# Attention and SoLU feed-forward on one core: a written order against an order set by a list schedule

## The chip, the core and the metric

The kernel runs on one core of a Trainium2 chip. A core has five engines, each with its own instruction queue worked strictly in order: TensorE (PE in the profile), VectorE (DVE), ScalarE (ACT), GpSimd (POOL) and SyncE (SP, which here only starts transfers). Engines wait for one another through semaphores; an instruction whose wait is not over holds up everything behind it on its engine. The metric is the device time of one execution in microseconds (us): 205.87 us in the median of three runs before the change (203.0 to 207.03).

## The reference

Attention over 4 batches of 8 heads (768 positions, 64 numbers per head), then a feed-forward block on the 3072 tokens of 512 numbers:

```python
scores = q @ k.T / sqrt(64) - slope[h] * dist     # kept: the last 96 positions and the first 8
a = softmax(scores);  x = a @ v                   # x as [3072, 512]
h = x @ w_in                                      # [3072, 1024]
solu = h * softmax(h)
ln = (solu - mean(solu)) / sqrt(var(solu) + 1e-6) * g_ln
out = ln @ w_out                                  # [3072, 512], float32
```

## The kernel before

The work is cut into 24 tiles of 128 tokens, six per batch. For a batch the q and k of two heads at a time (a pair, eight per batch) are loaded as float32 (`raw`), cast to fp16 by POOL (`qkn`, line 90), turned by six PE transposes into the PSUM bank `pt` (line 160) and copied out in order (`qkT`, line 164, q by DVE and k by ACT). Such a turn-and-copy is called a fill; there are 32. v is loaded per tile (`vst`) and cast by POOL (`vo`).

A tile n then goes through these steps. Scores of two halves on PE into `ps` (line 178), exp on ACT (`eb`, line 186; the first tile of a batch has half the width, line 189), times a mask on DVE (line 203), product with v on PE (`pav`, line 218), division by the sum on DVE (lines 233 and 237), four PE transposes (line 244) and a copy (`xT`). Feed-forward: eight 512-column matmuls on PE into `ph` (line 256), exp with row sum on ACT (`e`, line 268), `u = e*h` with row sum on DVE (line 274), a transposing transfer of u by SP (`uT`, line 279), squares with row sum on ACT (`sq`, line 285), five small POOL operations per two tiles for the factor `rs`, eight 512-column matmuls into `po` (line 308), scaling on ACT (`osb`, line 314), and the store, which ACT starts itself (line 316).

The mean of the normalisation is taken out of the weights beforehand: `gw_r = g * w_out` on ACT (line 323), its column mean by eight matmuls with a constant (`pm`, line 329), and `gw_sb = g * w_out - mean` on DVE (line 333). No `po` can start before that.

The order is written by hand: the loop over t at the end issues, for each t, the steps of several tiles in one fixed sequence (scores of t, feed-forward of t-2, output of t-4, store of t-5), with `gw_round` at t = 2 and 3, `gw_mean` and `gw_centre` at t = 4, and the fills of the next batch at the t that `FILLS` names. Loads of q, k and v are issued by SP, `w_in`, `w_out` and `g` by POOL (lines 356 to 359). PSUM has eight banks and all are taken: two each for `ps`, `pav` and `ph`, one for `pt` and one for `po`.

Of the kernel before, what the change touches and what calls it, by code (L numbers as in the profile page):

```python
# [9 lines left out]
FP32 = mybir.dt.float32  # L10
# [6 lines left out]
P = 128  # L17


@with_exitstack  # L20
def kernel(
# [24 lines left out]
    LAG = 4  # L46
# [14 lines left out]
    vo = const.tile([P, B, NA, H, D + 1], FP16, name="vo")  # L61
# [5 lines left out]
    vst = {}  # L67

    def load_v(n):
        b, a = divmod(n, NA)  # L70
        vst[n] = sb.tile([P, H, D], FP32, name="vst", bufs=4)
        nc.sync.dma_start(out=vst[n],
                          in_=v[b, :, ts(a, P), :].rearrange("h p d -> p h d"))

    def cast_v(n):
        b, a = divmod(n, NA)
        nc.gpsimd.tensor_copy(out=vo[:, b, a, :, 0:D], in_=vst.pop(n))  # L77

    raws, qkn = {}, {}

    def load_pair(b, w, pr):
        t = sb.tile([P, 2, NA * D], FP32, name="raw", bufs=10)
        nc.sync.dma_start(
            out=t, in_=(q, k)[w][b, 2 * pr : 2 * pr + 2].rearrange(
                "m (p a) d -> p m (a d)", a=NA))
        raws[b, w, pr] = t

    def cast_pair(b, w, pr):
        t = sb.tile([P, NA, 2, D], FP16, name="qkn", bufs=4)
        nc.gpsimd.tensor_copy(  # L90
            out=t.rearrange("p a m d -> p m a d"),
            in_=raws.pop((b, w, pr)).rearrange("p m (a d) -> p m a d", d=D))
        qkn[b, w, pr] = t

    with tc.manual_schedule():
        PAIRS = [(w, pr) for pr in range(NP) for w in range(2)]
        for i, (w, pr) in enumerate(PAIRS):
            load_pair(0, w, pr)
            if i == 3:
                load_v(0)  # L100
        load_v(1)
# [49 lines left out]
        qkT = {}  # L151

        def fill_pair(b, w, pr, tag="t"):

            if b not in qkT:
                qkT[b] = sb.tile([P, 2 * NP, S], FP16, name="qkT")
            pt = psum.tile([P, NA, P], FP16, name="pt", tag=tag)
            src = qkn.pop((b, w, pr))
            for a in range(NA):
                nc.tensor.transpose(  # L160
                    out=pt[:, a, :], in_=src[:, a].rearrange("p m d -> p (m d)"),
                    identity=ident)
            dst = qkT[b][:, w * NP + pr, :].rearrange("p (t a) -> p t a", a=NA)
            (nc.scalar.copy if w else nc.vector.tensor_copy)(  # L164
                out=dst, in_=pt.rearrange("p a t -> p t a"))

        ebs = {}

        def scores(n, half):
            b, a = divmod(n, NA)  # L170
            nb = 2 if a else 1
            ps = psum.tile([P, 2, 2, 2, P], FP32, name="ps", tag="s")
# [10 lines left out]
            eb = sb.tile([P, 2, 2, nb, P], FP16, name=f"eb{nb}", tag=f"eb{nb}", bufs=4)  # L183
            eb_f = eb.rearrange("p m s b f -> p (m s b f)")
            if nb == 2:
                nc.scalar.activation(out=eb_f, in_=ps.rearrange("p m s b f -> p (m s b f)"),  # L186
# [7 lines left out]
            if half == 1 and 1 <= a < NA - 1:  # L194

                nc.gpsimd.tensor_copy(out=qkT[b][:, NP : 2 * NP, ds(a * P, NG)],
                                      in_=qkT[b][:, NP : 2 * NP, 0:NG])
# [8 lines left out]

        pavs = {}

        def av(n, half):
# [5 lines left out]
            for i in range(4):  # L215
                m, slot = i % 2, i // 2
                for blk in range(nb):
# [3 lines left out]
                        rhs=vo[:, b, a - blk, 4 * half + i, :],  # L221
                        start=(i == 0 and blk == 0), stop=(i == 3 and blk == nb - 1),
                        skip_group_check=True)
            if half == 1 and 1 <= a < NA - 1:
                nc.gpsimd.tensor_copy(out=vo[0:NG, b, a], in_=vo[0:NG, b, 0])  # L225

        x16s, xTs = {}, {}
# [12 lines left out]
        def x_transpose(n):  # L240
            x16 = x16s.pop(n).rearrange("p g i d -> p (g i d)")
            pt = psum.tile([P, NCC, P], FP16, name="pt", tag="t")
            for c in range(NCC):
                nc.tensor.transpose(out=pt[:, c, :], in_=x16[:, ts(c, P)], identity=ident)
            xT = sb.tile([P, NCC, P], FP16, name="xT", bufs=3)
            nc.vector.tensor_copy(out=xT, in_=pt)
            xTs[n] = xT

        phs, es, us, uTs, sts, rss = {}, {}, {}, {}, {}, {}

        def ffn_in(n):
            xT = xTs.pop(n)
            ph = psum.tile([P, D_FF], FP32, name="ph", tag="h")
# [6 lines left out]
            phs[n] = ph  # L260

        def ffn_exp(n):
            if n % GT == 0:

                sts[n // GT] = stat.tile([P, 3, GT], FP32, name="st")
            i = n % GT
            es[n] = sb.tile([P, D_FF], FP16, name="e")
            nc.scalar.activation(out=es[n], in_=phs[n], func=AF.Exp,  # L268
                                 accum_out=sts[n // GT][:, 0, i : i + 1])

        def ffn_u(n):
            i = n % GT
            u = sb.tile([P, D_FF], FP16, name="u", bufs=3)
            nc.vector.scalar_tensor_tensor(  # L274
                out=u, in0=es.pop(n), scalar=1.0, in1=phs.pop(n),
                op0=ALU.mult, op1=ALU.mult,
                accum_out=sts[n // GT][:, 1, i : i + 1])
            uT = sb.tile([P, NFC, P], FP16, name="uT", bufs=LAG + 1)
            nc.sync.dma_start_transpose(out=uT, in_=u)
            us[n], uTs[n] = u, uT  # L280

        def ffn_sq(n):
            i = n % GT
# [167 lines left out]
```

## Time and profile before

| | before |
|---|---|
| profiled execution: time, span | 202.88 us, 201.1 us |
| busy: PE, PE weight loads | 148.8 us (74%), 81.0 us |
| busy: ACT, DVE, POOL | 131.9 us (66%), 115.5 us (57%), 83.9 us (42%) |
| moved by DMA | 34.85 MB, 173 GB/s in the mean |

How to read it: the span runs from the first to the last instruction, and the time of an execution has 1.8 us around it. Busy time is an average over stretches with different limits; the 40 digits of an engine cut the span in slices of 5.03 us, each digit the busy share in tenths. `PEclk` is the granted clock of TensorE in tenths of 2.4 GHz. The chain of waits follows the end of the span back: at each step to what released it, or to the instruction before it on its engine.

### The profile page before, as it was taken

The page shows a single profiled execution, that of the slowest core. Times are in us where ns is not written, and L with a number is a line of the kernel's source. Part 1 is how long each engine was busy: PE and PEld are TensorE (multiplying, and loading weights), DVE is VectorE, ACT ScalarE, POOL GpSimd, SP SyncE. Part 2 cuts the span into 40 slices and gives each one's busy share as a digit, 9 for nine tenths or more (in the row PEclk, how much of TensorE's full clock was granted, in tenths as well). Part 3 has the DMA queues.
Part 4 walks back from the last instruction along what each step waited for, and adds up shares of the span by engine and source line. Part 5 has one row for each costly group of instructions (what it writes and reads, how often), then busy time and mean ns, then how long its engine had stood idle before and what let it go on. Part 6 is the DMA issues. An engine that isn't in the chain of part 4 may idle for free.

```text
span 201.1 us, 3648 instructions
## 1 busy us (share of the span) xinstructions
PE 148.8 (74%) x1384; PEld 81.0 (40%) x1384; DVE 115.5 (57%) x194; ACT 131.9 (66%) x209; POOL 83.9 (42%) x170
## 2 busy tenths in 40 slices
PE   0565564394905778999699979987998899998742
PEld 0433332153402444555355545544554444543320
DVE  0324520346493568586689677767876667665300
ACT  4844222997230477789689868887897888885541
POOL 7786330546300346067443823747241243413020
PEclk9999999557885999999999999999999999999999
DMA  5999999998345046949977987585775534444442
GB/s 185 324 283 203 282 392 322 324 198 181 79 91 169 0 108 185 232 100 244 252 195 156 299 165 200 141 144 121 97 156 136 141 89 104 109 104 104 105 107 104
DMA packets 63570, 34.85 MB, mean 173 GB/s; under 512 B 51264, under 2 KB 59456, under 8 KB 63552
## 3 DMA queue, kind: packets, MB, share of 16 engines
q1 hardware_dynamic: 59008, 25.17, 55.3%
q10 hardware_dynamic: 3456, 6.29, 8.6%
q0 software_dynamic: 1088, 3.15, 5.8%
q8 instruction: 11, 0.18, 0.4%
q14 instruction: 7, 0.06, 0.1%
HBM read 23.07 MB, written 6.29 MB: 146 GB/s over the span
## 4 chain that ended last, share of the span: by engine, by line
ACT 34%; DVE 20%; PE 16%; DMA 16%; issue 6%; SPq 3%; ACTq 3%; POOL 1%; DVEq 0%; POOLq 0%
DVE u L274 14%; ACT e L268 13%; DMA g_sb<-in_moe_g_ln_dram 9%; ACT eb L186 6%; PE ph L256 6%; ACT osb L314 5%; ACT sq L285 5%; DMA raw<-in_q_dram 4%; DVE qkT L164 3%; ACTq L316 3%; PE po L308 3%; ACT gw_r L323 2%; DVE eb L203 2%; PE pt L160 2%; DMA raw<-in_k_dram 2%
## 5 line engine op out<-in xcount | busy, mean ns | idle before, releaser
L308 PE MATMUL po<-gw_sb,uT 128*128 128x512 f16 x192 | 46.7, 387 | 11.0 <-DMA raw<-in_k_dram 7.5
L256 PE MATMUL ph<-w_in_sb,xT 128*128 128x512 f16 x192 | 48.6, 399 | 0.6 <-DVE u L274 0.6
L186 ACT ACTIVATE eb<-ps 128x1024 f16<-128x1024 f32 x40 | 40.7, 1017 | 7.1 <-PE ps L178 7.1
L274 DVE SCALAR_TENSOR_TENSOR u<-e,ph 128x1024 f16<-128x1024 f16 x24 | 29.3, 1221 | 24.1 <-ACT e L268 24.0
L203 DVE TENSOR_TENSOR eb<-eb,mask 128x1024 f16<-128x1024 f16 (+1 forms) x48 | 37.4, 779 | 7.5 <-ACT eb L186 4.1
L285 ACT ACTIVATE sq<-u 128x1024 f16<-128x1024 f16 x24 | 25.4, 1058 | 12.6 <-DVE u L274 12.6
L268 ACT ACTIVATE e<-ph 128x1024 f16<-128x1024 f32 x24 | 24.6, 1023 | 13.4 <-PE ph L256 7.1
L160 PE MATMUL pt<-ident,qkn 128*128 128x128 f16 x192 | 18.8, 245 | 19.5 <-DVE qkT L164 9.9
L90 POOL CAST qkn<-raw 128x768 f16<-128x768 f32 x32 | 26.8, 838 | 7.6 <-DMA raw<-in_q_dram 5.0
L308 PEld LDWEIGHTS <-uT 128*128 128x128 f16 x192 | 17.7, 99 | 30.1 <-issue 13.3
L178 PE MATMUL ps<-qkT 64*128 64x128 f16 x352 | 20.4, 231 | 10.9 <-ACT eb L186 5.9
L256 PEld LDWEIGHTS <-xT 128*128 128x128 f16 x192 | 18.0, 102 | 20.2 <-issue 3.3
L164 ACT COPY qkT<-pt 128x768 f16<-128x768 f16 x16 | 12.7, 793 | 20.0 <-PE pt L160 20.0
L218 PE MATMUL pav<-vo,eb 128*128 128x65 f16 x352 | 20.4, 201 | 5.6 <-DVE eb L203 5.5
L160 PEld LDWEIGHTS <-qkn 128*128 128x128 f16 x192 | 14.2, 109 | 25.6 <-POOL qkn L90 11.6
L225 POOL COPY vo<-vo 8x520 f16<-8x520 f16 x16 | 11.7, 733 | 29.1 <-PE pav L218 28.9
L164 DVE COPY qkT<-pt 128x768 f16<-128x768 f16 x16 | 15.3, 955 | 14.1 <-PE pt L160 13.9
L293 POOL TENSOR_TENSOR t<-st 128x4 f32<-128x4 f32 x12 | 6.6, 547 | 34.5 <-DVE u L274 34.5
L218 PEld LDWEIGHTS <-eb 128*128 128x128 f16 x352 | 14.3, 101 | 12.7 <-DVE eb L203 9.1
L77 POOL CAST vo<-vst 128x512 f16<-128x512 f32 x24 | 15.6, 656 | 8.9 <-DMA vst<-in_v_dram 8.9
L314 ACT ACTIVATE osb<-po,rs 128x512 f32<-128x512 f32 x24 | 16.4, 683 | 4.0 <-PE po L308 2.0
L178 PEld LDWEIGHTS <-qkT 64*128 64x128 f16 x352 | 11.1, 98 | 18.6 <-issue 9.5
(43 smaller groups left out, 113.3 us busy)
## 6 DMA issues: line engine op xcount, KB each, us to landing
raw<-in_q_dram SPq DMA_DIRECT2D x16, 384.0 KB, 5.3
raw<-in_k_dram SPq DMA_DIRECT2D x16, 384.0 KB, 5.7
vst<-in_v_dram SPq DMA_DIRECT2D x24, 256.0 KB, 4.5
out_dram<-osb ACTq DMA_DIRECT2D x24, 256.0 KB, 2.5
w_out<-in_moe_w_out_dram POOLq DMA_DIRECT2D x1, 2048.0 KB, 17.9
w_in_sb<-in_moe_w_in_dram POOLq DMA_DIRECT2D x1, 1024.0 KB, 11.0
uT<-u SPq DMA_TRANSPOSE x24, 3.1
g_sb<-in_moe_g_ln_dram POOLq DMA_DIRECT2D x1, 4.0 KB, 17.3
```

The lines of the kernel that those rows point to most:

```text
L90: nc.gpsimd.tensor_copy(out=t.rearrange("p a m d -> p m a d"), in_=raws.pop((b, w, pr)).rearrange("p m (a d) -> p m a d", d=D))
L160: nc.tensor.transpose(out=pt[:, a, :], in_=src[:, a].rearrange("p m d -> p (m d)"), identity=ident)
L164: (nc.scalar.copy if w else nc.vector.tensor_copy)(out=dst, in_=pt.rearrange("p a t -> p t a"))
L178: nc.tensor.matmul(out=ps[:, m, slot, blk, :], lhsT=qkT[b][r, NP + pr, ts(a - blk, P)], rhs=qkT[b][r, pr, ts(a, P)], start=True, stop=True)
L186: nc.scalar.activation(out=eb_f, in_=ps.rearrange("p m s b f -> p (m s b f)"), func=AF.Exp, scale=inv_sqrt_d)
L203: nc.vector.tensor_tensor(out=eb.rearrange(pat), in0=eb.rearrange(pat), in1=mk.rearrange(pat if n % NA else "p m s f -> p (m s f)"), op=AL ...
L218: nc.tensor.matmul(out=pav[:, half, ds(i * (D + 1), D + 1)], lhsT=eb[:, m, slot, blk, :], rhs=vo[:, b, a - blk, 4 * half + i, :], start=(i ...
L256: nc.tensor.matmul(out=ph[:, ds(fh * 512, 512)], lhsT=xT[:, j, :], rhs=w_in_sb[:, j, ds(fh * 512, 512)], start=(j == 0), stop=(j == NCC - 1))
L268: nc.scalar.activation(out=es[n], in_=phs[n], func=AF.Exp, accum_out=sts[n // GT][:, 0, i : i + 1])
L274: nc.vector.scalar_tensor_tensor(out=u, in0=es.pop(n), scalar=1.0, in1=phs.pop(n), op0=ALU.mult, op1=ALU.mult, accum_out=sts[n // GT][:, 1 ...
L285: nc.scalar.activation(out=sq, in_=us.pop(n), func=AF.Square, scale=D_FF ** -0.5, accum_out=sts[n // GT][:, 2, i : i + 1])
L308: nc.tensor.matmul(out=po, lhsT=uT[:, c, :], rhs=gw_sb[:, c, :], start=(c == 0), stop=(c == NFC - 1))
```

## The change

A class `Plan` is added. Each step of the program is given to it as a task with the engines it may run on and a cost in us, a due time, the tasks it comes after, and the buffers it takes and frees. `run` picks again and again the engine and the task that can start earliest (within 0.15 us the one due first), books the model's time, and emits the instruction. So the program's order on each engine is that of the model's clock; on the chip nothing is decided at run time. The main parts of the diff:

```diff
+class Plan:
+    NEAR = 0.15
+    DEEP = 2.5
...
+    def ready(self, task, eng):
+        _, _, _, after, takes, _, load, _ = task
+        t = max(self.free[eng], self.dma - self.DEEP) if load else self.free[eng]
+        for a in after:
...
+            e, on = self.end[a]
+            t = max(t, e + (0.0 if on == eng else self.hop))
+        for r in takes:
...
+            t = max(t, self.rooms[r][0])
+        return t
...
-    LAG = 4
+    T = 5.4
+    LAG = 7
...
-    vo = const.tile([P, B, NA, H, D + 1], FP16, name="vo")
+    vo = const.tile([P, 2, NA, H, D + 1], FP16, name="vo")
...
+            rooms={"s": 1, "av": 1, "t": 1, "h": 1, "o": 1, "vst": 4, "raw": 10,
+                   "qkn": 4, "eb": 4, "x16": 2, "xT": 3, "e": 3, "u": 5, "ut": 5, "uT": LAG + 1,
+                   "osb": 3})
...
         def store(n):
...
-            nc.scalar.dma_start(out=out[ts(n, P), :], in_=osb)
...
+            nc.sync.dma_start(out=out[ts(n, P), :], in_=osbs.pop(n))
...
+        def load_g():
+            nc.sync.dma_start(out=g_sb, in_=moe_g_ln.rearrange("(j p) -> p j", p=P))
...
+        def load_w_out(i):
+            js = slice(2 * i, 2 * i + 2)
+            nc.sync.dma_start(out=w_out32[:, js],
+                              in_=moe_w_out.rearrange("(j p) c -> p j c", p=P)[:, js])
...
+                add(("qc", *x), {gp: 0.86, ve: 0.85} if b == 0 else {gp: 0.86},
+                    lambda e, x=x: cast_pair(*x, e), due - 0.5 * T,
+                    after=[("ql", *x)], takes=("qkn",), frees=("raw",))
...
+                add(("qo", *x), {ve: 0.95, sc: 0.75}, lambda e, x=x: order_pair(*x, e),
+                    due, after=[("qt", *x)], frees=("t",))
...
+                add(("m", n, h), {ve: 0.35 if z else 0.65}, lambda e, n=n, h=h: mask_mul(n, h),
+                    sh + 0.2, after=[("e", n, h)])
...
+            add(("o", n), {"PE": 1.75}, lambda e, n=n: ffn_out(n), s + LAG * T,
+                after=[("ut", n)] + [("gc", j) for j in range(NFC)], takes=("o",), frees=("uT",))
+            add(("os", n), {sc: 0.72, ve: 0.72}, lambda e, n=n: scale_out(n, e), s + 2 * T,
+                after=[("o", n), ("pw", g)], takes=("osb",), frees=("o",))
...
+        add("w_in", {gp: 1.2}, lambda e: load_w_in(), -37.0, load=5.4, lag=1.0,
+            after=[("qc", 0, 1, 1)])
+        add("g", {"SP": 0.3}, lambda e: load_g(), -25.0, load=0.5, lag=1.0)
+        for i in range(4):
+            add(("wl", i), {"SP": 0.3}, lambda e, i=i: load_w_out(i), 1.5 * T + i * T,
+                load=1.45, lag=1.0)
+        for j in range(NFC):
+            add(("gr", j), {sc: 0.62, ve: 0.62, gp: 0.75}, lambda e, j=j: gw_round(j, e),
+                4 * T + 0.5 * j * T, after=[("wl", j // 2), "g"])
+            add(("gc", j), {ve: 0.68}, lambda e, j=j: gw_centre(j), 6 * T + 0.2 * j * T,
+                after=["gm"], frees=("o",) if j == NFC - 1 else ())
+        add("gm", {"PE": 1.75}, lambda e: gw_mean(), 5.5 * T,
+            after=[("gr", j) for j in range(NFC)], takes=("o",))
+        plan.run()
```

Beside these, `e` has 3 buffers where it had 2, `u` 5 where it had 3, `uT` 8 where it had 5; the fills of the first batch use the bank of `pt` alone, where they also used that of `po`; the rounded weights go into `gw_sb` itself; `vo` keeps two batches; the factor `rs` of the last tiles is made tile by tile, with its sums on DVE.

Three places in the order. ACT at the exp of tile 0 (`e`; `eb` are exps of scores, the COPY is a fill's), before:

```order
L186 ACTIVATE eb_323<-ps 128x1024
L186 ACTIVATE eb_360<-ps 128x1024
L323 ACTIVATE gw_r<-w_out_69,g_sb 128x512 x4
L268 ACTIVATE e,st<-ph 128x1024
L186 ACTIVATE eb_411<-ps 128x1024
L285 ACTIVATE sq,st<-u 128x1024
```

and now:

```order
L286 ACTIVATE eb_282<-ps 128x1024
L286 ACTIVATE eb_311<-ps 128x1024
L256 COPY qkT<-pt 128x768
L369 ACTIVATE e,st<-ph 128x1024
L286 ACTIVATE eb_386<-ps 128x1024
L256 COPY qkT<-pt 128x768
L383 ACTIVATE sq,st<-u 128x1024
```

The four roundings of weights stood ahead of the first `e`; now the first of them stands behind it, and the eight are spread over ACT (3), DVE (3) and POOL (2).

POOL at the loads of the weights, before:

```order
L90 CAST qkn<-raw 128x2x6x64 x4
L77 CAST vo<-vst 128x8x64
L90 CAST qkn<-raw 128x2x6x64 x3
L356 DMA w_in_sb<-in_moe_w_in_dram 128x4x1024
L90 CAST qkn<-raw 128x2x6x64
L358 DMA w_out_69<-in_moe_w_out_dram 128x8x512
L359 DMA g_sb<-in_moe_g_ln_dram 128x8x1
```

and now:

```order
L199 MEMSET meanw 128x128
L240 CAST qkn<-raw 128x2x6x64 x2
L431 DMA w_in_sb<-in_moe_w_in_dram 128x4x1024
L222 CAST vo<-vst 128x8x64
L260 COPY qkT<-qkT 128x4x8
```

The load of `w_in` stands behind two casts instead of eight (DVE does six of the first batch's eight q and k casts); `w_out` and `g` are SP's, `w_out` in four pieces.

SP in the middle of the program, before:

```order
L279 DMA_TRANSPOSE uT<-u 128x8x128
L83 DMA raw<-in_q_dram 128x2x384
L83 DMA raw<-in_k_dram 128x2x384
L72 DMA vst<-in_v_dram 128x8x64
L279 DMA_TRANSPOSE uT<-u 128x8x128
```

and now:

```order
L379 DMA_TRANSPOSE uT<-u 128x8x128
L422 DMA out_dram<-osb 128x512
L217 DMA vst<-in_v_dram 128x8x64
L422 DMA out_dram<-osb 128x512
L233 DMA raw<-in_q_dram 128x2x384
L233 DMA raw<-in_k_dram 128x2x384
L379 DMA_TRANSPOSE uT<-u 128x8x128
```

The stores, which ACT started from its own queue, stand between SP's loads and transposing transfers.

## Rows read from the trace of the kernel before

**Rows 1.** The page: busy time of each engine, then PE's digits and granted clock

```profile
PE 148.8 (74%) x1384; PEld 81.0 (40%) x1384; DVE 115.5 (57%) x194; ACT 131.9 (66%) x209; POOL 83.9 (42%) x170
...
PE   0565564394905778999699979987998899998742
...
PEclk9999999557885999999999999999999999999999
```

**Rows 2.** Chain of waits, start to tile 4: start us, length us, what

```profile
16.52 17.34 DMA g_sb<-in_moe_g_ln_dram
...
36.50 1.01 ACT e L268 x2
...
62.37 3.25 PE po L308 x8
...
77.11 1.12 ACT e L268 x2
```

**Rows 3.** Chain of waits, one round of a later tile, and the last `e`

```profile
102.03 0.59 ACT osb L314
102.64 0.34 ACTq L316
103.03 1.12 ACT e L268 x2
104.17 1.24 DVE u L274 x2
105.44 0.96 ACT sq L285
106.49 1.00 ACT eb L186
107.50 0.59 ACT osb L314
...
188.62 1.12 ACT e L268 x2
```

**Rows 4.** Timeline of PE: start us, length us, engine, line, tile, shape, count

```profile
120.61 0.39 PE L244 MATMUL pt<-ident,x 128*128 128x128 f16 x4
...
120.93 0.40 PE L178 MATMUL ps<-qkT 64*128 64x128 f16 x8
...
121.26 0.42 PE L218 MATMUL pav<-vo,eb 128*128 128x65 f16 x8
...
121.51 1.89 PE L308 MATMUL po<-gw_sb,uT 128*128 128x512 f16 x8
...
123.24 0.50 PE L160 MATMUL pt<-ident,qkn 128*128 128x128 f16 x6
...
123.67 0.40 PE L178 MATMUL ps<-qkT 64*128 64x128 f16 x8
```

**Rows 5.** Timeline: load of w_in, first ph, a slow mask, last po

```profile
13.88 0.97 POOL L356 DMA_DIRECT2D w_in_sb<-in_moe_w_in_dram  x1
...
27.84 3.46 PE L256 MATMUL ph<-w_in_sb,xT 128*128 128x512 f16 x8
...
50.33 1.61 DVE L203 TENSOR_TENSOR eb<-eb,mask 128x1024 f16<-128x1024 f16 x1
...
195.52 1.89 PE L308 MATMUL po<-gw_sb,uT 128*128 128x512 f16 x8 [0.82 <-ACT osb L314]
```

**Rows 6.** Groups of instructions on DVE: busy us, mean ns, idle before

```profile
L203 DVE TENSOR_TENSOR eb<-eb,mask 128x1024 f16<-128x1024 f16 (+1 forms) x48 | 37.4, 779 | 7.5 <-ACT eb L186 4.1 <-ACT eb L189 2.6
...
L237 DVE TENSOR_TENSOR x<-pav,rl 128x512 f16<-128x512 f32 x24 | 16.6, 692 | 0.8
...
L164 DVE COPY qkT<-pt 128x768 f16<-128x768 f16 x16 | 15.3, 955 | 14.1 <-PE pt L160 13.9
```

**Rows 7.** Transfers: issuing queue, count, KB each, median us from issue to landing

```profile
out_dram<-osb ACTq DMA_DIRECT2D x24, 256.0 KB, 2.5
...
w_in_sb<-in_moe_w_in_dram POOLq DMA_DIRECT2D x1, 1024.0 KB, 11.0
```

More of the change, by code (lines that the diff above doesn't have):

```diff
@@ L1 @@
+import heapq
 import math
@@ L171, in scores @@
             nb = 2 if a else 1
-            ps = psum.tile([P, 2, 2, 2, P], FP32, name="ps", tag="s")
+            ps = pss[n, half] = psum.tile([P, 2, 2, 2, P], FP32, name="ps", tag="s")
             for slot in range(2):
@@ L259, in ffn_in @@
                         start=(j == 0), stop=(j == NCC - 1))
-            phs[n] = ph
-        def ffn_exp(n):
[L263 to L269, printed above, removed]
+        groups = [[n + i for i in range(GT)] for n in range(0, NT - GT, GT)]
@@ new lines, with sums @@
+        groups += [[n] for n in range(NT - GT, NT)]
+        place = {n: (g, i) for g, ns in enumerate(groups) for i, n in enumerate(ns)}
+        def sums(n, what):
+            g, i = place[n]
+            if g not in sts:
+                sts[g] = stat.tile([P, 3, len(groups[g])], FP32, name="st")
+            return sts[g][:, what, i : i + 1]
+        def ffn_exp(n):
+            acc = sums(n, 0)
+            es[n] = sb.tile([P, D_FF], FP16, name="e", bufs=3)
+            nc.scalar.activation(out=es[n], in_=phs[n], func=AF.Exp, accum_out=acc)
@@ new lines @@
+        add = plan.add
+        BT = NA * T
+        for b in range(B):
+            for i, (w, pr) in enumerate(PAIRS):
+                x = (b, w, pr)
+                due = b * BT - (NP * 2 - i) * (0.8 * BT / 8) if b else -40.0 + 2 * i
+                add(("ql", *x), {"SP": 0.3}, lambda e, x=x: load_pair(*x), due - 3 * T,
+                    takes=("raw",), load=1.1, lag=1.0)
+                add(("qc", *x), {gp: 0.86, ve: 0.85} if b == 0 else {gp: 0.86},
+                    lambda e, x=x: cast_pair(*x, e), due - 0.5 * T,
+                    after=[("ql", *x)], takes=("qkn",), frees=("raw",))
+                last = [("s", NA * (b - 1) - 1, 1)] if b > 1 else []
+                add(("qt", *x), {"PE": 0.43}, lambda e, x=x: turn_pair(*x), due,
+                    after=[("qc", *x)] + last, takes=("t",), frees=("qkn",))
+                add(("qo", *x), {ve: 0.95, sc: 0.75}, lambda e, x=x: order_pair(*x, e),
+                    due, after=[("qt", *x)], frees=("t",))
```

366 lines of the change are left out of this document (202 added, 164 removed).

## The prediction, as it was put on record

> **What bounds the kernel now.** I read the page first. PE is the busiest engine, 148.8 us of 201.1, and its digits split the span [rows 1]: up to the 13th slice (65 us) they are mostly 3 to 6 with two nines and a zero, then 7 to 9, and they fall in the last three. So there are three stretches, with different limits. I cut them at the exp of the feed-forward, `e`, of tiles 0, 4 and 23, because the chain of waits passes through each: 36.50, 77.11 and 188.62 us [rows 2, 3].
>
> Start to `e` of tile 0, 36.5 us. The chain holds one link of 17.34 us, the landing of `g` [rows 2]. `g` is queued on POOL behind the 2 MB of `w_out`, and ACT's order has four roundings that need it ahead of the first `e`. PE had the first `ph` ready at 27.84 + 3.46 = 31.3 [rows 5], so ACT held `e` for 5 us behind work that was not urgent.
>
> Tiles 0 to 4, 77.11 - 36.50 = 40.6 us, or 10.2 per tile. Here the reader is to see what does not belong to a tile: the second four roundings, the mean, eight centrings in a row on DVE, and the first `po`, 3.25 us at 62.37 for eight matmuls that take 1.73 later [rows 2, 4]. The granted clock is half (1.2 GHz) in slices 8, 9 and 13, behind slices in which PE's digits are 4 and 0 [rows 1].
>
> Tiles 4 to 23, 111.5 us, or 5.87 per tile. One round of the chain, from `osb` at 102.03 to the next at 107.50, is 5.47 us and goes through ACT and DVE in written order: `osb`, the start of the store (0.34), `e`, `u`, `sq`, `eb` [rows 3]. PE's own work per tile, by start-to-start times [rows 4]: `po` 123.24 - 121.51 = 1.73; `ph` has the same eight matmuls, 1.73; scores 0.33 and product 0.25, each twice; the turn of x 0.32; that is 4.94. A fill is 0.43. The 19 tiles need 93.9, less 0.58 for each of the three that begin a batch (half width), plus 16 fills: 99.0 us of 111.5, or **88.8%**. So PE is already near its limit there and cannot gain much.
>
> **The change, part by part.**
>
> Start. The lists of ACT and POOL show the two edits that count. No rounding stands ahead of the first `e`, so the link of 17.34 goes; what is late next is `w_in`. Its issue stands behind two q and k casts on POOL instead of eight casts. It was issued at 13.88 and took 11.0 to land [rows 5, 7]. The seventh pair's cast stood ahead of it; now the second of POOL's two casts needs the fifth pair. By proportion that is 13.88 x 5/7 = 9.9, and no sooner is the upper end, 13.88; I take 10.7, as the first load takes its time whatever follows: landed at 21.7. A cold `ph` of 3.46 ends at 25.3. ACT still has a copy and two `eb` of tile 2 ahead of `e`. Lower bound 25.3; upper bound 31.3, where `ph` ended before. I take the middle, **28.5**, since both the earlier load and the work ahead of it are real. The single bank for the first fills costs nothing here as long as `w_in` is later than they are; without that cover it is up to a copy (0.955, [rows 6]) for each of eight fills, 7.6 us less what the loads' own pace hides, about the width of the bounds.
>
> Tiles 0 to 4. The steps are the same, but spread: the roundings over three engines, the centrings between other DVE work, the first `po` much later (due seven tiles after its own). I count what now stands on each engine between `e` of tile 0 and of tile 4. ACT: eight full `eb` at 1.01 and two half ones, four `e` at 1.14, four `sq` at 1.05 (starts in [rows 3]), five copies (at most 0.955), three roundings (at most 1.01): 8.1 + 1.0 + 4.6 + 4.2 + 4.8 + 3.0 = 25.7. DVE between `u` of tile 0 and of tile 4: four `u` at 1.27, ten masks at 0.779, two copies at 0.955, and 22 smaller ones (norms, x copies, three roundings, four centrings) at no more than 0.692 [rows 3, 6]: 5.1 + 7.8 + 1.9 + 15.2 = 30.0 at most. So 24 to 30 if these engines are kept full, 40.6 if nothing is won. PE needs only four `ph` and some five tiles of scores and eight fills, about 18. I take **28**, near the engine sums, because no load is waited for here any more: the weights' pieces are asked for from the second tile on.
>
> Tiles 4 to the last `po`. PE now owes more: all 24 `po` (41.5), 19 `ph` (32.9), 17 tiles of scores and products at 1.16 less two halves of 0.58 (18.6), 19 turns of x (6.1), 15 fills (6.5): 105.6 us. Before, three `po` were done by then. ACT loses the 0.34 of the store's start and six of 24 `osb`; DVE gains these six (about 0.692 each, the row with the same shapes) and twelve small sums of the last tiles, which hide behind the last turn of u. Neither is the bound: their busy times, 131.9 and 115.5, come out near 126 each, below PE's. So I keep PE's 88.8%: 105.6 / 0.888 = **118.9**. Bounds: 97%, that is 108.9, if PE is never without work; 84.5%, that is 125, if the new order fits less well than the old.
>
> End. After the start of the last `po` the old kernel needs 201.1 - 195.52 = 5.6 [rows 5], of which 1.73 is in PE's sum: 3.9. The transposing transfer of the last u is waited for with nothing else left for PE; I put 3.0 for it, more than the 2.5 of a store [rows 7]. Together **6.9**.
>
> The stores cost SP a start each, 24 times 0.34 [rows 3], on a queue that mostly waits; their landing can come later than 2.5. Three `osb` buffers and one store per tile leave two tiles, over 10 us, before that reaches `po`, so I cost it at nothing; if that cover goes, each tile waits on its store. The trace has the stores on a queue of their own. The Trainium skill (DMA: Bandwidth & Descriptors, Queues, rings and completion order) says that each DMA engine takes turns between the queues it has work for; by that a store on SP's queue loses its own turn and stands behind the loads ahead of it. No run here shows a store on that queue; by the rule the sum would only change once a store took over 10 us.
>
> Masks: 0.779 in the mean, but 1.61 at 50.33 [rows 5, 6], so something on the chip stretches them that the plan's 0.65 doesn't have. The Trainium skill (SBUF — State Buffer, Who interferes with whom) says that DVE and GpSimd share a pair of ports under an exclusive lock, which DVE copies and casts in their two-port modes and two-input operations can take, and that GpSimd then cannot write its descriptors for a transfer. By that rule six casts on DVE beside the issue of `w_in` speak against this change: up to 3 us on the start.
>
> Sum: 28.5 + 28 + 118.9 + 6.9 = 182.3 us of span, against 201.1. The start gives 8.0, tiles 0 to 4 give 12.6, the rest takes back 1.8. The profiled execution took 202.88, 1.78 more than its span: 184.1. The median of the runs shown, 205.87, is 3.0 above the profiled execution, so I forecast **187 us**.
>
> **The rivals.** A difference under 2% (201.8 to 210.0) can't be told from no change here.
>
> 1. Forecast: the start is won, then PE is the bound at 86 to 93%. 177 to 194 us. Chance 0.62.
> 2. PE is never without work after tile 4 (97%) and the engines are full before it (24): 28.5 + 24 + 108.9 + 6.9 = 168.3, 173 us. For: two to three more buffers and ACT and DVE at some 70%. Against: one bank each for `po` and `pt`, two for `ph`, as before, each released by ACT or DVE. Chance 0.08.
> 3. The start is won by half. `w_in` lands late (the transfers of the first 36 us are what the loads of two batches and the weights share, or the ports' lock delays it), `e` of tile 0 comes at 33, tiles 0 to 4 take 36: 33 + 36 + 118.9 + 6.9 = 194.8, so 199.6. For: the loads are the same in number, and the mask row of 1.61 shows an engine held up. Against: `ph` was done at 31.3 even with `w_out` in the way. Chance 0.15.
> 4. The order is of the model's clock and the chip's is another: an engine stands at a task that is not ready while ready ones are behind it. Its place is DVE between the masks, `u` and the centrings, where 0.65 is planned and 0.779 to 1.61 occurs. If nothing is won in tiles 0 to 4 (40.6), the kernel is slower than 210 from the point at which PE falls to 105.6 / (205.2 - 28.5 - 40.6 - 6.9) = 82%; at 75%, 140.8 us, the time is 216.8 + 4.8 = 222. For: due times with no slack for a late step. Against: waits of a fraction of a us per tile are covered by two or more tiles in flight, and the hand-written order has 88.8% too. Chance 0.07, and 0.08 for ending between, at 201.8 to 210.
> 5. It doesn't do what its words say. By the lists, casts go elsewhere only in the first batch (six), copies are 18 on ACT and 14 on DVE instead of 16 and 16, six `osb` move. So the placing is nearly the old one, and balancing would bring nothing where PE bounds; the order is all there is. This changes no number above, since I count nothing for balance.
>
> **The numbers.** Faster by over 2%: cases 1 to 3, 0.85; within: 0.08; slower: 0.07. The range takes case 1 and 3 with the bounds of start (25.3 to 31.3), tiles 0 to 4 (24 to 36) and efficiency: **177 to 200**.
>
> **What would show it.** `e` of tile 0 at 25 to 31 us, with `w_in` and not `g` in the chain; `e` of tile 4 at 52 to 61; then 5.8 to 6.3 us per tile, PE's digits at 9 there, and its first `po` after 55 us. The granted clock is full from about 30 us on. The masks keep a mean near 0.78. I am wrong on the start if `e` of tile 0 comes after 33; wrong on the bound if after tile 4 PE is below 85% while ACT or DVE is above; and wrong on the queue if `po` waits for `osb` buffers or for `uT` in the middle of the program.

## The result, and the profile after

The changed kernel takes 185.86 us (median of four runs, 184.51 to 186.68) against 206.45 (203.0 to 207.66) of the kernel before, timed with it: 0.9085 of its time [0.8941, 0.9229]. A later repeat gave 186.08 against 204.55, 0.9137 [0.907, 0.9204]. Times here are medians of all executions, while the ratios and their 95% intervals leave out executions that fell in a slower state, so a ratio is not the quotient of the two medians. The forecast was 187 us. The profiled execution took 186.13 us with a span of 184.4; before it was 202.88 and 201.1.

Cut where the prediction cuts, at `e` of tiles 0, 4 and 23:

| stretch | before | forecast | after |
|---|---|---|---|
| start to `e` of tile 0 | 36.4 us | 28.5 | 28.8 |
| to `e` of tile 4 | 40.7 | 28 | 29.8 |
| to `e` of tile 23 (19 tiles) | 111.5 | - | 112.6 |
| to the end | 12.5 | - | 13.3 |
| `e` of tile 4 to the end | 124.0 | 125.8 | 125.9 |
| whole span | 201.1 | 182.3 | 184.4 |

So 7.6 us come from the start and 10.9 from tiles 0 to 4, and what follows takes 1.9 back. The `e` of tiles 0 and 23, from ACT's timeline:

```profile
28.77 1.02 ACT L369 ACTIVATE e<-ph 128x1024 f16<-128x1024 f32 x1 [1.64 <-PE ph L349]
...
171.10 1.02 ACT L369 ACTIVATE e<-ph 128x1024 f16<-128x1024 f32 x1 [0.92 <-PE ph L349]
```

The chain's shares of the span by engine were, before:

```profile
ACT 34%; DVE 20%; PE 16%; DMA 16%; issue 6%; SPq 3%; ACTq 3%; POOL 1%; DVEq 0%; POOLq 0%
```

The page of the kernel after, with the rows that answer to [rows 1] and the chain's shares by engine and line:

```profile
PE 147.2 (80%) x1384; PEld 83.1 (45%) x1384; DVE 119.1 (65%) x219; ACT 126.3 (69%) x200; POOL 79.2 (43%) x157
...
PE   0337478686779799999999899799998799988581
...
PEclk9999999789969999999999999999999999999955
...
PE 52%; DVE 12%; ACT 11%; issue 9%; DMA 6%; POOL 6%; SPq 1%; POOLq 0%
PE ph L349 20%; PE po L406 15%; PE pt L248 5%; PE pav L313 5%; PE ps L275 4%; DVE u L373 4%; DMA raw<-in_k_dram 4%; ACT eb L286 3%; DVE eb L300 3%; ACT qkT L256 3%; DMA uT<-u 2%; DVE qkT L256 2%; ACT sq L383 2%; DVE x L328 2%; ACT e L369 2%
```

PE's digits rise earlier than before and then stand at 9; the link of 17.34 us to `g` [rows 2] is gone. A slice is 4.6 us now. The granted clock has new low slices at the very end.

The chain at the start, where the prediction expected `w_in` (start us, length us, what):

```profile
2.24 7.10 DMA raw<-in_k_dram
...
12.53 0.81 PE pt L248 x6
...
13.37 0.81 ACT qkT L256
...
14.22 0.81 PE pt L248 x6
...
26.29 2.44 PE ph L349 x8
```

Turn, copy, and the next turn: 1.69 us per fill (12.53 to 14.22), each turn waiting until the copy before it has emptied the one bank `pt`. `w_in` was issued at 11.31, landed at 21.1, and nobody waited for it. From there to tile 4 the chain has:

```profile
34.90 3.35 PE ph L349 x8
...
46.95 3.27 POOL gw_sb L444 x2
50.22 0.57 POOL vo L226
50.78 0.79 POOL qkn L240
...
51.61 0.82 PE pt L248 x6
...
58.54 0.03 ACT e L369
```

The second `ph` runs at half clock (1.2 GHz granted from 34.4 to 37.8 us), behind 1.09 us without work on PE: 3.35 in place of 1.73. Two roundings on POOL take 1.64 us each, where the plan has 0.75, and a cast that a fill waits for is queued behind them.

Busy time by stretch (from:to, its length, then PE, weight loads, DVE, ACT, POOL with the count of instructions, granted clock, share of the DMA engines, GB/s):

```profile
28.80:58.50 29.70, 22.43 (x258) 14.05 (x256) 23.60 (x41) 22.61 (x34) 20.37 (x33) 0.89 0.97 242
...
65.00:93.00 28.00, 27.66 (x257) 15.29 (x257) 21.66 (x38) 20.81 (x34) 14.97 (x30) 1.00 1.16 277
93.00:120.00 27.00, 25.10 (x249) 14.28 (x247) 18.63 (x33) 19.20 (x30) 14.97 (x28) 1.00 0.78 165
120.00:171.10 51.10, 47.40 (x436) 24.98 (x434) 35.15 (x72) 39.97 (x64) 12.56 (x30) 1.00 0.43 98
171.10:184.40 13.30, 6.18 (x16) 1.89 (x16) 2.52 (x7) 2.95 (x5) 0.55 (x1) 0.62 0.38 82
```

PE is busy for 99% of 65 to 93 us and 93% afterwards. The share of the DMA engines is full too in both stretches shown up to 93 us (0.97 and 1.16), and 0.43 after 120. What answers to [rows 4] and [rows 5] at the end, from PE's timeline:

```profile
173.33 2.61 PE L406 MATMUL po<-gw_sb,uT 128*128 128x512 f16 x8 [2.27 <-DMA uT<-u]
176.83 3.57 PE L406 MATMUL po<-gw_sb,uT 128*128 128x512 f16 x8 [0.90 <-DVE osb L418]
```

PE waits 2.27 us for a transposing transfer, its granted clock is half from 174.4 on, and the last `po` takes 3.57 us where before it took 1.89 [rows 5]. The masks (724 ns in the mean for 779) and the transfers of [rows 6, 7] have changed little; the turns of u come beside them:

```profile
L300 DVE TENSOR_TENSOR eb<-eb,mask 128x1024 f16<-128x1024 f16 (+1 forms) x48 | 34.3, 724 | 9.1 <-ACT eb L290 4.8
...
out_dram<-osb SPq DMA_DIRECT2D x24, 256.0 KB, 2.5
...
uT<-u SPq DMA_TRANSPOSE x24, 3.4
...
w_in_sb<-in_moe_w_in_dram POOLq DMA_DIRECT2D x1, 1024.0 KB, 9.8
```

### The profile page after: what moved, and what is told of

The parts are those of the page before. It is cut to its first block, busy times and chain, and to the rows that moved or that the text cites. A ratio compares the mean times of both kernels' runs of the same rounds, so it can differ in the third digit from the quotient of the medians.

```text
span 184.4 us, 3669 instructions
## 1 busy us (share of the span) xinstructions
PE 147.2 (80%) x1384; PEld 83.1 (45%) x1384; DVE 119.1 (65%) x219; ACT 126.3 (69%) x200; POOL 79.2 (43%) x157
## 4 chain that ended last, share of the span: by engine, by line
PE 52%; DVE 12%; ACT 11%; issue 9%; DMA 6%; POOL 6%; SPq 1%; POOLq 0%
PE ph L349 20%; PE po L406 15%; PE pt L248 5%; PE pav L313 5%; PE ps L275 4%; DVE u L373 4%; DMA raw<-in_k_dram 4%; ACT eb L286 3%; DVE eb L300 3%; ACT qkT L256 3%; DMA uT<-u 2%; DVE qkT L256 2%; ACT sq L383 2%; DVE x L328 2%; ACT e L369 2%
## 5 line engine op out<-in xcount | busy, mean ns | idle before, releaser
L406 PE MATMUL po<-gw_sb,uT 128*128 128x512 f16 x192 | 47.8, 394 | 3.5 <-DMA uT<-u 2.6
L300 DVE TENSOR_TENSOR eb<-eb,mask 128x1024 f16<-128x1024 f16 (+1 forms) x48 | 34.3, 724 | 9.1 <-ACT eb L290 4.8
L240 POOL CAST qkn<-raw 128x768 f16<-128x768 f32 x26 | 21.8, 847 | 17.1 <-PE pt L248 10.4
L248 PEld LDWEIGHTS <-qkn 128*128 128x128 f16 x192 | 15.2, 110 | 21.1 <-issue 8.7
L416 ACT ACTIVATE osb<-po,rs 128x512 f32<-128x512 f32 x18 | 12.4, 686 | 14.3 <-issue 6.4
L313 PE MATMUL pav<-vo,eb 128*128 128x65 f16 x352 | 18.6, 197 | 2.7 <-DVE eb L300 1.5
L256 ACT COPY qkT<-pt 128x768 f16<-128x768 f16 x18 | 14.4, 799 | 8.5 <-PE pt L248 8.5
L222 POOL CAST vo<-vst 128x512 f16<-128x512 f32 x24 | 17.4, 729 | 5.9 <-DMA vst<-in_v_dram 4.0
L256 DVE COPY qkT<-pt 128x768 f16<-128x768 f16 x14 | 13.3, 953 | 9.8 <-PE pt L248 9.8
L226 POOL COPY vo<-vo 8x520 f16<-8x520 f16 x16 | 9.7, 609 | 19.6 <-PE pav L313 19.6
L328 DVE TENSOR_TENSOR x<-pav,rl 128x512 f16<-128x512 f32 x24 | 16.6, 692 | 0.8
```

The source lines that it names most:

```text
L240: ENG[eng](out=t.rearrange("p a m d -> p m a d"), in_=raws.pop((b, w, pr)).rearrange("p m (a d) -> p m a d", d=D))
L248: nc.tensor.transpose(out=pt[:, a, :], in_=src[:, a].rearrange("p m d -> p (m d)"), identity=ident)
L256: ENG[eng](out=dst, in_=pts.pop((b, w, pr)).rearrange("p a t -> p t a"))
L300: nc.vector.tensor_tensor(out=eb.rearrange(pat), in0=eb.rearrange(pat), in1=mk.rearrange(pat if n % NA else "p m s f -> p (m s f)"), op=AL ...
L313: nc.tensor.matmul(out=pav[:, half, ds(i * (D + 1), D + 1)], lhsT=eb[:, m, slot, blk, :], rhs=vo[:, b % 2, a - blk, 4 * half + i, :], star ...
L406: nc.tensor.matmul(out=po, lhsT=uT[:, c, :], rhs=gw_sb[:, c, :], start=(c == 0), stop=(c == NFC - 1))
```

## The experiments

All are timed against the kernel before on the chip they ran on; ratios are to it. The changed kernel itself was not timed again beside runs 5, 6, 8 and 9: they are set against its 185.86 and 186.08 us, and differences of 1 us cannot be told there. What is read from a trace is one execution of each run.

**1. The late weights and late outputs by hand, without the list schedule.** The kernel before, with the roundings, the mean and the centrings at later t and the outputs caught up:

```diff
-            if t in (2, 3):
-                for j in range(4 * t - 8, 4 * t - 4):
+            if t in (5, 6):
+                for j in range(4 * t - 20, 4 * t - 16):
...
-            if t == 4:
+            if t == 7:
...
-            if has(t - LAG):
-                ffn_out(t - LAG)
+            for n in range(NT):
+                if last_out(t) == n:
+                    ffn_out(n)
```

> The old hand-written order with one thing moved: the roundings, the mean and the centrings of the weights stand three tiles later, and the first outputs seven tiles behind their tile, caught up to four by tile 10. Theory A (the gain is the weights' work leaving the first five tiles): the link on g goes, e of tile 0 at 27 to 30, e of tile 4 near 57, then the old 5.87 us per tile plus four late po: 186 to 191 us. Rival B (the hand-written order of the rest is what costs): start and tiles 0 to 4 get shorter as under A, but tiles 4 to 23 get longer by what the late po add between the old waits, 125 us and more: 194 to 200.

213.42 us (212.78 to 215.01), 1.0521 [1.0378, 1.0663]: slower than before, in size neither theory, in kind B. `e` of tile 0 came at 32.5, so the link to `g` was indeed worth 4 us. Tile 4 came at 69.5, 7.6 us sooner than before but far behind the 57 of theory A; then the gain went: tile 6 at 94.0 against 89.7, and tiles 4 to 23 took 129.9 us for 111.5. Its chain in the early tiles:

```profile
20.68 16.69 DMA vst<-in_v_dram
...
40.08 3.42 PE ph L256 x8
...
43.52 1.12 ACT e L268 x2
44.67 1.23 DVE u L274 x2
...
49.32 3.43 PE ph L256 x8
```

A load of v takes the place of the link to `g`, and then there is one serial round of 9.2 us from `ph` to `ph`, with `ph` at half clock (slices of the granted clock at 5). The work on the weights was moved but not spread, and it is paid for between tiles 5 and 6, 14.6 us for 5.5: eight centrings in a row on DVE, 5.3 us, for which PE waits before the first `po`, again at half clock (PE's timeline):

```profile
87.70 3.57 PE L308 MATMUL po<-gw_sb,uT 128*128 128x512 f16 x8 [7.50 <-DVE gw_sb L333]
```

Late weights and outputs alone are not the gain. That the schedule's order gains because it spreads this work and fills the early tiles fits both traces, but no run changes only that.

**2. Two banks for the first fills, known to the plan.**

```diff
+        def bank(b, w, pr):
+            return "o" if b == 0 and PAIRS.index((w, pr)) % 2 else "t"
...
-            pt = pts[b, w, pr] = psum.tile([P, NA, P], FP16, name="pt", tag="t")
+            tag = "o" if bank(b, w, pr) == "o" else "t"
+            pt = pts[b, w, pr] = psum.tile([P, NA, P], FP16, name="pt", tag=tag)
...
-                    after=[("qc", *x)] + last, takes=("t",), frees=("qkn",))
+                    after=[("qc", *x)] + last, takes=(bank(*x),), frees=("qkn",))
```

> The changed kernel, with the first batch's fills alternating between the banks of pt and po as before the change. In its trace the chain of the first 25 us is turn, copy, turn, copy through one bank, 1.69 us each. Theory A (this chain sets the end): e of tile 0 comes 3 to 4 us sooner and the end with it, 182 to 183 us. Rival B (what comes after is set by something else that does not start sooner): e of tile 0 sooner, the time within 1 us of 185.9.

189.29 us (187.85 to 189.94), 0.9311 [0.9172, 0.945]. `e` of tile 0 came 3.9 us sooner, at 24.90, but tile 6 at 69.63 against 67.64. The plan had made another order, and in it the chain waits for loads:

```profile
53.59 4.71 DMA raw<-in_q_dram
...
60.45 6.58 DMA vst<-in_v_dram
...
67.70 3.69 POOL qkn L240 x3
```

So bank and order were mixed here; run 10 parts them.

**3. The old places under the new order's rules.** Casts on POOL, q copies on DVE and k copies on ACT, `osb` and roundings on ACT:

```diff
-                add(("qc", *x), {gp: 0.86, ve: 0.85} if b == 0 else {gp: 0.86},
+                add(("qc", *x), {gp: 0.86},
...
-                add(("qo", *x), {ve: 0.95, sc: 0.75}, lambda e, x=x: order_pair(*x, e),
+                add(("qo", *x), {sc: 0.75} if w else {ve: 0.95}, lambda e, x=x: order_pair(*x, e),
...
-            add(("os", n), {sc: 0.72, ve: 0.72}, lambda e, n=n: scale_out(n, e), s + 2 * T,
+            add(("os", n), {sc: 0.72}, lambda e, n=n: scale_out(n, e), s + 2 * T,
```

> The list schedule with no free choice of engine: all casts on POOL, q copies on DVE, k copies, osb and roundings on ACT, as before the change. Theory A (the placing is nearly the old one and brings nothing): 185 to 187 us. Rival B (the free choice matters at a few places where ACT would be waited for): 189 to 193 us.

189.33 us (189.16 to 189.84), 0.9327 [0.923, 0.9424], so with the old places 3.4 us are lost, in the range of B. Not where one would look: `e` of tile 4 came at 49.8, sooner than with free placing; then the centrings came in runs of four and three on DVE and the first `po` ran at half clock (61.60, 3.50 us), and at tile 21 the two are level, 160.95 and 160.57. The loss is at the end (`e` of tile 22 at 170.50 for 166.38), where PE waits for DVE and then for a turn of u, and the matmuls behind run at half clock (PE's timeline):

```profile
167.17 3.29 PE L349 MATMUL ph<-w_in_sb,xT 128*128 128x512 f16 x8
...
177.43 3.31 PE L406 MATMUL po<-gw_sb,uT 128*128 128x512 f16 x8 [2.08 <-DMA uT<-u]
```

The plan's order changes with the places, so the two are not parted here.

**4. Less work on PE.** Two of eight matmuls of each `po` left out: 24 times 0.43, 10.4 us of PE's work. The edit, with `stop` moved to the last that is left:

```diff
-            for c in range(NFC):
+            for c in range(NFC - 2):
```

> The changed kernel in the same order, leaving out two of the eight matmuls of each po: 24 x 2 x 0.2165 = 10.4 us less work on PE, nothing else. Theory A (PE is the bound after tile 4): 8 to 10 us less, 176 to 178 us. Rival B (PE is busy but the rounds through ACT, DVE and the fixed order are as long): 1 to 4 us less, 182 to 185 us.

182.51 us (181.75 to 184.23), 0.8974 [0.8837, 0.9112]. A third of the 10.4 us came back. In the profiled execution, the longest of the four, `e` of tile 11 was 3.1 us sooner (97.92 for 100.99), tile 13 was later (117.50 for 116.95), tile 23 the same (171.12 for 171.10). The chain shows what came instead:

```profile
89.08 5.63 DMA vst<-in_v_dram
...
96.66 4.64 DMA vst<-in_v_dram
...
103.70 3.53 PE ph L349 x8
...
140.46 4.74 DMA uT<-u
```

A load of v, POOL's cast behind it, PE without work for 1.66 us and then a `ph` at half clock; later the turn of u. The row of v's casts on the page (busy us, mean ns, idle before and what ended it):

```profile
L222 POOL CAST vo<-vst 128x512 f16<-128x512 f32 x24 | 17.3, 724 | 16.7 <-DMA vst<-in_v_dram 16.4
```

POOL waits 16.4 us for v's loads; in the changed kernel it waits 4.0.

**5. Half of v's load.**

```diff
-            nc.sync.dma_start(out=vst[n],
-                              in_=v[b, :, ts(a, P), :].rearrange("h p d -> p h d"))
+            nc.sync.dma_start(out=vst[n][:, 0:4],
+                              in_=v[b, 0:4, ts(a, P), :].rearrange("h p d -> p h d"))
```

> The order of the changed kernel, instruction for instruction; each load of v fetches four of the eight heads (half the bytes and half the packets), and the cast on POOL writes these four into both halves, so POOL's, PE's, ACT's and DVE's work keep their sizes. Part of the input is left out, so the output is not the reference's. What is asked: what sets the 5.9 us per tile after tile 4, now that less work on PE did not shorten it. Theory D, the transfers: the DMA engines are 97 to 99% busy up to 120 us; 24 halves at about 1.35 us of all 16 engines is 16 us less, some 10 of it between 29 and 106 us. Then exp of tile 4 comes 1 to 3 us sooner, tile 13 (116.95) 4 to 8 us sooner, the whole takes 178 to 182 us. Theory R, the rounds ph, e, u, sq and ps, eb, mask, pav in a fixed order through PE, ACT and DVE: the loads are ahead of their need, so no more than 1 us falls: 185 to 187.

185.37 us (184.32 to 186.91), 0.9087 [0.9027, 0.9146]; tile 13 at 117.58. Half of v's load alone brings nothing that can be told from the noise; the loads of q and k and the turns of u were not lightened.

**6. Less work on ACT.**

```diff
-            nc.scalar.activation(out=sq, in_=us[n], func=AF.Square,
+            nc.scalar.activation(out=sq[:, 0:P], in_=us[n][:, 0:P], func=AF.Square,
```

> The order of the changed kernel, instruction for instruction; the square of u on ACT goes over 128 of its 1024 columns (the sum of squares is then that of an eighth of the row: part of the computation is left out). That is about 0.85 us less on ACT per tile, 20 us in all, 16 of it between tile 4 and 23, on nothing but ACT. Theory R (rounds in a fixed order; ACT, PE and DVE each have about 5 us of work per tile with the time between starts): the rounds that pass through ACT get shorter by up to 0.85 us where sq stands in the chain: 3 to 10 us in all, 176 to 183. Theory D (transfers): within 1 us, 185 to 187. The old theory P (PE alone) says the same as D here, 185 to 187, but the leaving out of PE's work has already spoken against it.

185.41 us (184.03 to 187.04), 0.9067 [0.9012, 0.9121]. ACT is busy 109.5 us in place of 126.3, and no `e` moved by more than 0.5 us. Less `sq` brings nothing, so ACT's load is not a limit here.

**7. Both 4 and 5.**

> Two of eight matmuls of each po left out, as once before (there: 182.5 us, exp of tile 13 at 117.50), together with half of each load of v, as once before (185.4 us, 117.58; changed kernel 116.95). Each of them alone moved exp of tile 13 by nothing. In the run with less PE work the chain between 84 and 104 us went through loads of v that landed 4.6 to 5.6 us after their issue, then through POOL to the scores, and PE fell to half clock. Theory L (two limits lie within 4 us of each other there, PE first and the loads behind it): with both eased exp of tile 13 comes at 109 to 113, the whole takes 175 to 179. Theory X (the fixed order has rounds that depend on neither): exp of tile 13 at 116 or later, 181 to 183.

180.95 us (179.16 to 181.99), 0.8847 [0.8779, 0.8915], between the theories on the whole time and close to L on the place it was made for, ACT's timeline at tile 13:

```profile
113.52 1.02 ACT L372 ACTIVATE e<-ph 128x1024 f16<-128x1024 f32 x1 [2.10 <-PE ph L352]
```

In these executions each edit alone moved this `e` by nothing (0.6 us later), both together by 3.4 us, of the 13 x 0.43 = 5.6 that PE has less to do by then; POOL's wait for v's loads fell from 16.4 us in run 4 to 3.0. That fits two limits close together, PE first, v's loads with POOL's cast right behind. In the whole time the two edits come near to a plain sum: 3.6 and 0.7 us alone, 5.1 together. So the two limits are read at this place, in one execution of each run, and the medians do not show them by themselves.

**8. The last two turns of u on PE.**

```diff
+            else:
+                add(("up", n), {"PE": 0.5}, lambda e, n=n: turn_u_pe(n), s, after=[("u", n)],
+                    takes=("t", "uT"), frees=("ut",))
+                add(("ut", n), {ve: 0.9}, lambda e, n=n: copy_u(n), s, after=[("up", n)],
+                    frees=("t",))
```

> The changed kernel, with u of the last two tiles turned by eight transposes on PE each (into the bank of the fills, then two copies on DVE) in place of the transposing transfer (3.1 us from issue to landing). In the changed kernel po of tile 22 waits 2.27 us for that transfer, PE's granted clock falls to half from 174.4 us on, and the last po takes 3.57 us for eight matmuls that take 1.89 at full clock. Theory T: the tail is short of this transfer and of the clock that falls while PE waits for it: the last po starts at 173 to 174.5 instead of 176.83 and takes 1.9; 181 to 182.5 us in all. Rival: what is late next, sq, its four small sums and the power for the last osb, takes the place: 184 to 185.5.

183.44 us (182.62 to 183.96), 0.8988 [0.8943, 0.9032], against 186.08 for the changed kernel repeated (run 11). 0.9 us above the upper end of theory T. PE's timeline:

```profile
174.75 0.62 PE L386 MATMUL pt<-ident,u 128*128 128x128 f16 x8 [0.75 <-DVE u L373]
175.89 1.90 PE L419 MATMUL po<-gw_sb,uT 128*128 128x512 f16 x8 [0.52 <-ACT sq L396]
```

The last `po` starts only 0.94 us sooner than 176.83, since `ph` of tile 23 now stands behind the turn of u of tile 22 (its `e` at 172.32 for 171.10), but it takes 1.90 for 3.57: most of the difference between these two executions is the clock. Against the repeated changed kernel, whose clock stayed full (run 11), the last `po` starts 0.6 us sooner and takes the same.

**9. The stores back on ACT's queue.**

```diff
-            nc.sync.dma_start(out=out[ts(n, P), :], in_=osbs.pop(n))
+            nc.scalar.dma_start(out=out[ts(n, P), :], in_=osbs.pop(n))
```

> The changed kernel with its 24 stores issued by ACT, where they stood before the change, at the same places of the order; nothing else is moved. The prediction counted the move to SP's queue at nothing, beside 0.34 us less on ACT per tile. Theory N (nothing hangs on it): ACT has room, 185 to 187. Theory S (on SP's queue a store holds up the turns of u and the loads behind it, 0.5 us each, up to 2.86 for two): without them the turns start sooner, 182 to 184.5. Theory Q (ACT is in the rounds, so 24 times 0.34 to 0.5 us come back on it): 188 to 193.

188.75 us (186.73 to 190.52), 0.9231 [0.9164, 0.9299], against 0.9137 [0.907, 0.9204] for the changed kernel: 2 to 3 us slower, in the range of theory Q but not by its mechanism. Run 6 took more off ACT than these stores put on it, and nothing came back. In the profiled execution (the longest of six) `e` stays 0.3 to 0.5 us behind the changed kernel's from tile 0 to tile 15, where theory Q would add 0.34 with every tile; then it falls behind in steps, to 1.9 us at tile 23, and PE waits for turns of u before `po`, 5.8 us in four waits (2.6 in two in the changed kernel). The page shows what goes with these waits (count, KB, median us to landing):

```profile
out_dram<-osb ACTq DMA_DIRECT2D x24, 256.0 KB, 3.4
...
uT<-u SPq DMA_TRANSPOSE x24, 3.8
```

Stores and turns of u both land later than in the changed kernel (2.5 and 3.4), and so do the loads of v (5.7 for 5.0). One of the waits, from PE's timeline:

```profile
141.07 1.90 PE L406 MATMUL po<-gw_sb,uT 128*128 128x512 f16 x8 [0.71 <-DMA uT<-u]
```

The rest of the loss is in the tail, where a store and a turn of u overlap. The transfers issued between 170 and 173 us, and the `po` behind:

```profile
out_dram<-osb ACTq DMA_DIRECT2D x1, 256.0 KB, 5.2
uT<-u SPq DMA_TRANSPOSE x1, 5.9
```

```profile
176.70 3.59 PE L406 MATMUL po<-gw_sb,uT 128*128 128x512 f16 x8 [3.71 <-DMA uT<-u]
```

By this trace the stores cost by what they do to the other transfers, not by ACT's time. Why transfers land later when two queues hold them, no run tells.

**10. Two banks under the changed kernel's order.** Only the bank alternates, the plan is told of one:

```diff
+            tag = "o" if b == 0 and PAIRS.index((w, pr)) % 2 else "t"
```

> The changed kernel with the fills of the first batch turned into two banks in alternation, t and o, while the plan is still told of one: so the order on every engine is the changed kernel's, instruction for instruction, where the run with two banks that the plan knew of had another order (e of tile 0 at 24.90 in place of 28.77, but e of tile 6 at 69.63 in place of 67.64, and 189.3 us). Theory O (it was the other order of the loads that lost there): e of tile 0 at 24.5 to 26.5, tile 4 at 54 to 57, and 181.5 to 184 us. Theory W (what is won at the start is waited for later whatever the order, because the transfers are full until 120 us): e of tile 4 at 57.5 to 59, 185 to 187 us.

181.64 us (180.72 to 184.1), 0.8907 [0.884, 0.8975]: theory O. `e` of tile 0 at 25.7, tile 4 at 55.6, and the 3 us won at the start stay to tile 13 (114.16 for 116.95). What was lost in run 2 was lost by its other order.

**11. Both 8 and 10, and the changed kernel once more.**

> The same two banks under the changed kernel's order, with the last two tiles' u turned by PE as well (that alone: 183.4 us). If both gains add, 179 to 181.5; by theory W 183 to 184.5, the tail's gain alone. If it holds, it is faster than both kernels.

> The changed kernel once more, unaltered, on the chip of these runs, so that differences of 1 to 3 us can be told: 185 to 187 us.

179.68 us (179.41 to 181.9), 0.8828 [0.8769, 0.8886], beside 186.08 (184.13 to 187.45), 0.9137 [0.907, 0.9204], for the changed kernel. The gains nearly add (4.4 and 2.6 us alone, 6.4 together), and this version beats both kernels. PE's timeline at its start, two fills (12 transposes) in one go:

```profile
9.84 1.44 PE L249 MATMUL pt<-ident,qkn 128*128 128x128 f16 x12 [0.73 <-DVE qkT L257]
...
14.73 1.47 PE L249 MATMUL pt<-ident,qkn 128*128 128x128 f16 x12
...
22.05 3.03 PE L350 MATMUL ph<-w_in_sb,xT 128*128 128x512 f16 x8
```

`w_in` was issued at 10.31 here and took 9.9 to land, so it was there at 20.2, 1.8 us before this first `ph`: still not what is waited for, but near.

The repeated changed kernel waits at its end as the first did, but at full clock in the profiled execution (span 182.4):

```profile
173.35 1.90 PE L406 MATMUL po<-gw_sb,uT 128*128 128x512 f16 x8 [2.35 <-DMA uT<-u]
176.52 1.90 PE L406 MATMUL po<-gw_sb,uT 128*128 128x512 f16 x8 [1.27 <-DMA uT<-u]
```

## Why the prediction came out right, step by step

**The sum: two misses that cancel.** The span was 184.4 us for 182.3 forecast. The 3.0 us that the forecast adds because the median lay above the profiled execution before did not come again (185.86 for 186.13). That 187 was met to 1.1 us is in part luck.

**The start: the size right, the step wrong.** 28.8 for 28.5, by chance. The prediction put `w_in` next in line and so costed the single bank at nothing "as long as `w_in` is later than they are". It was not: it landed at 21.1, near the estimate (21.7; issued 0.6 us later, landed in 9.8 for 11.0), and the first `ph` began at 26.09 behind the fills. The cover that the step named was missing, and by runs 10 and 11 the bank costs 3.0 to 3.7 us. The prediction had bounded this (up to 7.6 us less what the loads hide) and then took the other case. The rule of the Trainium skill on the shared ports (SBUF — State Buffer, Who interferes with whom) was held against the change at up to 3 us on the start, a size for which the prediction gives no working. The issue took 1.12 us, 0.97 before [rows 5], but only one of DVE's six casts ran beside it (11.53 to 12.09 us), so the rule was hardly put to the test. By the same section of the Trainium skill an operation with two inputs in SBUF hinders only GpSimd's reads, so for the writing of descriptors the prediction should have named copies and casts alone. POOL's roundings at 1.64 us for a planned 0.75 may be that lock; no run tells.

**Tiles 0 to 4: nearly right.** 29.8 for 28. But the engines were not full, as "near the engine sums" has it: DVE, ACT and PE were each busy 76 to 79% of this stretch. The intervals that stand out are 9.5 us (tiles 0 to 1, a wait for a copy of x and then a `ph` at half clock) and 10.7 (tiles 3 to 4, POOL's two roundings, then the mean). In run 1 the weights and outputs, moved late in the written order, won 3.7 us of this stretch (37.0 for 40.7) and lost more behind it.

**Tile 4 to the last `po`: the number right to 0.7 us, the bound half right.** The sum counts PE's stretch to the end of the last `po`, without the wait for the last turn of u, which it puts into the end. The last `po` ends at 176.83 + 3.57 = 180.40. Cut so, the stretch is 180.40 - 58.54 - 2.27 = 119.6 us for 118.9, and 105.6 us of PE's work in it is 88.3%, for 88.8 assumed. PE does set the pace to 100 us or so: run 4 won 2.7 us between tiles 4 and 11. But 10.4 us less of its work brought 3.6 in all. Runs 4, 5 and 7 point to v's loads as the next limit, less than 4 us away; and after 120 us `e` of the last ten tiles came at nearly the same pace with and without that work (53.6 us from tile 13 to 23 for 54.2). There the chain of run 4 shows u, its turn of 4.7 us and `po`; no run shortened that alone, so this last limit is read, not shown. PE had 16% of the chain of waits before and has 52% now, so the two orders are not limited alike, and that the old divisor of 88.8% fits the new one is in part luck. (By `e` of tile 4 before, two `po` were done and not three; the sum does not use it.)

**The end: right to 0.6 us**, 184.4 - 180.40 + 2.27 = 6.3 for 6.9 by the same cut, with 2.27 waited for the transposing transfer where 3.0 were put. That PE's clock can fall in this wait was not in it: the sign that the granted clock is full from about 30 us on is wrong at 34.4, 51.5 and 174.4 us. Of the other signs, `w_in` never came into the chain, and `po` did wait for `uT` in the middle of the program, but once and for 0.32 us.

**Case 5, placing counts for nothing: not borne out.** With the old places the time is 3.4 us more (run 3), most of it in the last two tiles. The copies look nearly alike in a count, 18 and 14 for 16 and 16; by which of them, and whether through the order that the plan then makes, no run says. **Stores on SP at nothing: right**, and better by 2 to 3 us (run 9). The 0.34 us of ACT per tile [rows 3] had been a link of the old round, but run 9 shows the gain elsewhere: in how soon the transfers land. The rule that the prediction weighed, that engines take turns between queues (the Trainium skill, DMA: Bandwidth & Descriptors, Queues, rings and completion order), speaks for a queue of its own. The stores land in 2.5 us in the median on ACT's queue before [rows 7] and on SP's queue after; under the new order on ACT's queue it is 3.4 (run 9). A queue of its own brought nothing here.

**The rivals.** The third (start won by half) put the chance on `w_in`, which was not it. The fourth, an order of the model's clock that is not the chip's, occurred in small on POOL and not on DVE: two roundings of 1.64 us, planned at 0.75, stand ahead of a cast that a fill waits for (tiles 3 to 4). Run 2 shows how much hangs on the order: a change of one bank gave another one and 3.4 us more.

## What to carry to other kernels

A share of 90% on one engine does not say that its work sets the time: take 10 us of it away and see what returns, then ease the next limit with it, and compare whole times as well as one place in one trace. A result inside a theory's range is not yet its mechanism: run 9 came out in theory Q's range for another reason. When a step is costed at nothing because something else is later, work out both times, here fills at 1.69 us each against the landing of `w_in`. With a list schedule an edit changes the order as well, so test the edit once under the old order before blaming it.

## What the runs showed of the hardware

- A wait on PE can cost twice: behind waits of 1.1 to 7.5 us the eight matmuls of a `po` or `ph` took 3.3 to 3.6 us at half clock, 1.89 else. It is not the same each time. The wait for the turn of u in the tail (2.3 to 2.5 us) was followed by half clock at the last `po` in the changed kernel and runs 6 and 10, and by full clock in run 5 and in the repeated changed kernel. That this widens the spread of times is not shown: six runs lay within 1.4 us without the wait (run 8), but within 2.5 in the version of run 11 that lacks it too, and within 3.3 with it.
- A transposing transfer of u landed in 3.0 to 3.1 us when alone. In the tail of the changed kernel it took 4.5 with a store issued 1.3 us behind it on the same queue, yet two others with the same store at the same distance (issued at 135.96 and 157.70) took 3.1, so the store is not shown to be the cause. In run 9 it took 5.9 with a store on ACT's queue 0.4 us later, and the median of all 24 rose from 3.4 to 3.8.
- A float32 cast of 128x768 took 0.58 us on DVE and 0.85 on POOL; a rounding with a scale, 128x512, 0.83 on DVE (median) and 1.64 on POOL.
- Even with the two banks, SP's issue of the load of `g` (4 KB) took 2.9 to 3.8 us and that of the q load behind it 3.2, against 0.45 for the first loads. A k load of 384 KB issued later took 4.3 in the changed kernel, so the small load is not shown to be the cause. To move it is the next thing to try at the start.
